# Constant rows of a packed attention operand: from fill transfers to the evacuation itself, for the first two head groups

## The chip, the cores and the metric

One core of a Trainium2 chip runs the kernel. The metric is the device time of one execution in microseconds (us). Executions that the records call fast are compared with fast ones only.

How a ratio is computed: it is the mean time of one kernel's fast runs over that of the kernel before's fast runs of the same rounds, so it is not quite the ratio of the medians that are quoted.

Engines: PE is TensorE (PEld its weight loads), ACT is ScalarE, DVE is VectorE, POOL is GpSimd, SP is SyncE, which issues all DMA transfers here (SPq is its queue).

## The reference, cut to what matters

```python
# S = 2048 tokens, D = 512, H = 32 heads of 16, F = 1792
def reference(A_x, A_wqkv, A_wo, B_x, B_w1, B_w3, B_w2):
    ...
    xn = _layernorm(A_x)
    return A_x + _A_ref(xn, A_wqkv, A_wo) + _B_ref(xn, B_w1, B_w3, B_w2)
# _A_ref: softmax attention over 2048 x 2048 scores in each of 32 heads, then the output projection wo
# _B_ref: the gated feed-forward part (FFN): (silu(xn w1) * (xn w3)) w2
```

The expensive part is 32 x 2048 x 2048 exponentials. They come in 2,048 *score tiles*, each of 128 keys by 512 queries of one head.

## The kernel before

**Layout.** Each head has 16 dimensions, but the matmuls of this kernel take their rows in places of 32. So the transposed keys `KT` and queries `QT` keep four heads in 128 rows: in each place of 32, rows 0 to 15 hold the head, row 16 a constant (1 in `QT`, an offset `YB` in `KT`), and rows 17 to 31 zeros. There are eight such groups of four heads. The offset lets DVE make an exponential out of integer bit operations. ACT makes the other exponentials, three tiles at a time. About a fifth of the tiles (398 of 2,048) go to DVE.

**Fills.** Constants and zeros get into their rows by DMA, from small source rows:

```python
        P.dma(lambda e: e.dma_start(KT[16:128:32, :, :]..., crow[:, 1, :].unsqueeze(1).broadcast_to([4, NG * NQC, 512])),
              reads=[("crow",)], writes=[("KTc",)], kb=128)
        def zeros(g0, g1):
            for j in range(4):
                P.dma(lambda e, j=j: e.dma_start(                                        # L1114
                    KT[32 * j + 17:32 * j + 32, g0:g1, :].rearrange("p g (a n) -> p (g a) n", n=512),
                    zrow[:, :].unsqueeze(1).broadcast_to([15, (g1 - g0) * NQC, 512])),
                    reads=[("zrow",)], writes=[("KTz", g) for g in range(g0, g1)], kb=60 * (g1 - g0))
        for j in range(4):
            P.dma(lambda e, j=j: e.dma_start(QT[32 * j + 17:32 * j + 32, :, :], ...      # L1119
        zeros(0, 2)
        P.post("sp", lambda: [zeros(g, g + 2) for g in range(2, NG, 2)], ready=14.0, prio=2)
```

**Packing moves.** A projection computes 128 dense rows, that is, eight heads. DVE copies them to a staging tile `stg`, and eight transfers of 16 rows carry them to their places:

```python
                def moves(hh):
                    for j in range(4):
                        m = P.dma(lambda e, j=j: e.dma_start(dst(hh)[32 * j:32 * j + 16, :],   # L1303
                                      stg[64 * hh + 16 * j:64 * hh + 16 * j + 16, sl, :]), ..., kb=16)
```

**The end of a unit.** A unit is one group of heads with one chunk of 512 queries, 64 score tiles; there are 32. At its end the sums of the exponentials are fetched by a transfer (`Lc`), inverted on DVE (`Rc`), and spread over the rows by more transfers.

```python
            def e1():
                q = P.dma(lambda e: e.dma_start(Lc[:, u, :], U[16:128:32, us, :]), ...)
                P.post("dve", e2, ready=q.end + _LAT, prio=0)
            ...
            def e2():
                q = P.op("dve", lambda e: e.reciprocal(Rc[:, :], Lc[:, u, :]), reads=[("Lc", u)], writes=[("Rc",)],
                         dur=0.25)                                                       # L1760
                P.post("sp", e3, ready=q.end + _LAT, prio=0)
```

**The order.** The program itself places every instruction in its engine's queue, by a list scheduler that works at build time with assumed durations (`dur`) and a clock `P.t` that steps by 0.02 us. A task is put into an engine's queue when the *model* says that its data will have come, and a transfer is assumed to take 0.06 us of the issuing queue:

```python
    def dma(self, fn, reads=(), writes=(), kb=64, name="", eng="sp"):
        op = _Prog.dma(self, fn, reads, writes, name, eng)
        return self._time(op, op.deps, 0.06, 1.9 + kb / 200.0)   # 0.06 us to issue, then latency
    ...
            P.t += 0.02
```

## Time and profile before

| what | value |
|---|---|
| time, median of the first 3 runs | 1001.12 us (999.04 to 1002.58) |
| span of the profiled run, mean granted clock | 998.7 us, 0.898 |
| first score matmul | 44.2 us |
| time at score tile 128 | 152.2 us |
| time at score tile 513 (first of the second query chunk) | 318.1 us |
| tiles 513 to 2048 | 640.2 us |

From the page of the kernel before: busy time by engine, the 40 slices (a digit is a busy share in tenths, for PEclk the granted clock), the chain that ended last, and two rows of the DMA issues (KB each, us from issue to landing).

```profile
span 998.7 us, 21498 instructions
PE 830.9 (83%) x8925; PEld 251.3 (25%) x8925; DVE 761.5 (76%) x1498; ACT 802.8 (80%) x736; POOL 55.0 (6%) x73
...
PE   3264758897987989698989999889999999898991
...
ACT  4233759797998979699998999888898999988940
...
PEclk9595879899987999899996999998886999998996
...
PE 37%; DVE 30%; ACT 13%; DMA 11%; SPq 7%; issue 2%; POOL 0%; DVEq 0%
...
f_KT<-f_stg SPq DMA_DIRECT2D x128, 16.0 KB, 1.8
...
f_KT<-f_mb SPq DMA_DIRECT2D x16, 120.0 KB, 3.4
```

The first six slices, 150 us, are thin on PE and ACT alike. From there on both are 90% full or near it. By windows (start:end and length; busy time with instruction count of PE, PEld, DVE, ACT and POOL; clock; DMA share; GB/s). The trace has no clock record before 16.5 us, and the view counts time without a record as full clock, so the clock of the first 50 us is read too high.

```profile
0.00:50.00 50.00, 15.38 (x158) 6.29 (x162) 20.10 (x52) 15.53 (x16) 11.43 (x39) 0.77 0.40 99
50.00:100.00 50.00, 28.48 (x356) 9.67 (x348) 18.47 (x33) 17.30 (x21) 1.08 (x3) 0.75 0.42 63
150.00:550.00 400.00, 351.45 (x3648) 99.95 (x3646) 335.71 (x661) 357.51 (x326) 20.94 (x15) 0.92 0.24 31
```

The chain of waits of the kernel before says what the early time goes into (start, length, what):

```profile
24.87 3.33 DMA f_KT<-f_mb
28.22 3.34 DMA f_KT<-f_mb
31.58 3.35 DMA f_KT<-f_mb
34.94 0.87 SPq L1114
```

The timeline of the same stretch (start, length, engine, line, operation; in brackets the idle time before it and what ended it) shows who stands behind these transfers:

```profile
24.87 10.94 SPq L1114 DMA_DIRECT2D f_KT<-f_mb  x4
...
35.85 5.02 SPq L1303 DMA_DIRECT2D f_KT<-f_stg  x8
40.92 5.01 SPq L1303 DMA_DIRECT2D f_QT<-f_stg  x8
44.20 1.06 PE L1536 MATMUL ps<-f_QT,f_KT 32*128 32x512 bf16 x5 [20.03 <-DMA f_QT<-f_stg]
...
45.98 27.69 SPq L1114 DMA_DIRECT2D f_KT<-f_mb  x10
```

The keys were staged by 20.5 us, but their eight moves sit in the SP queue behind the zero fills and start at 35.85. Then 16 moves take 10 us of queue. PE is empty for 20 us. After the first scores the next ten fills hold the queue for another 27.7 us.

### The profile page before, as it was taken

How to read it: one execution, taken by the hardware profiler on the slowest of the kernel's cores; microseconds unless marked ns; L12 is line 12 of the kernel's file. 1: busy time of each engine (PE TensorE's matmuls, PEld its weight loads, DVE VectorE, ACT ScalarE, POOL GpSimd, SP SyncE). 2: the span in 40 equal slices, each digit the busy share in tenths (PEclk: the TensorE clock that was granted, in tenths of full speed). 3: DMA queues.
4: the chain of work that ended last, by engine and by line, in shares of the span. 5: the costliest groups of instructions: out<-in, count | busy, mean ns of one | idle time of the engine just before them, and what ended most of it. 6: DMA issues, size and time to landing. Idle time of an engine off the chain costs nothing.

```text
span 998.7 us, 21498 instructions
## 1 busy us (share of the span) xinstructions
PE 830.9 (83%) x8925; PEld 251.3 (25%) x8925; DVE 761.5 (76%) x1498; ACT 802.8 (80%) x736; POOL 55.0 (6%) x73
## 2 busy tenths in 40 slices
PE   3264758897987989698989999889999999898991
PEld 1021212222221232122221222222222222222261
DVE  5243759797898778598988969878898889886942
ACT  4233759797998979699998999888898999988940
POOL 3100001000000000000000000000000000000000
PEclk9595879899987999899996999998886999998996
DMA  5234322140321222231511131413321222333112
GB/s 161 38 43 81 95 34 39 20 57 23 51 21 9 22 23 35 33 45 24 68 16 6 11 37 17 42 36 52 44 29 12 29 23 30 43 43 46 16 24 31
DMA packets 93294, 37.67 MB, mean 38 GB/s; under 512 B 74756, under 2 KB 91140, under 8 KB 93188
## 3 DMA queue, kind: packets, MB, share of 16 engines
q1 hardware_dynamic: 93188, 36.21, 26.1%
q8 instruction: 72, 1.18, 0.5%
q14 instruction: 34, 0.28, 0.1%
HBM read 22.81 MB, written 2.10 MB: 25 GB/s over the span
## 4 chain that ended last, share of the span: by engine, by line
PE 37%; DVE 30%; ACT 13%; DMA 11%; SPq 7%; issue 2%; POOL 0%; DVEq 0%
PE ps L1536 13%; PE ps L1228 13%; ACT f_PT L1573 12%; PE ps L1725 11%; DVE f_yb L1623 10%; SPq L1303 6%; DVE f_xd L1668 5%; DMA f_KT<-f_mb 4%; DVE f_mb L1657 3%; DVE f_xd L1651 3%; DVE f_xd L1662 3%; DVE f_t L1370 2%; DMA f_Lc<-f_U 2%; DMA f_QT<-f_mb 1%; DVE f_hT L1380 1%
## 5 line engine op out<-in xcount | busy, mean ns | idle before, releaser
L1573 ACT ACTIVATE f_PT<-ps 128x1536 bf16<-128x1536 f32 (+1 forms) x660 | 767.0, 1292 | 134.9 <-PE ps L1536 126.3
L1536 PE MATMUL ps<-f_QT,f_KT 32*128 32x512 bf16 x2048 | 336.7, 412 | 86.2 <-DVE f_yb L1623 26.4
L1623 DVE TENSOR_SCALAR f_yb<-ps 128x512 int16<-128x512 f32 x398 | 271.5, 684 | 58.2 <-PE ps L1536 54.8
L1725 PE MATMUL ps<-f_PT,f_Vaug 128*32 128x512 bf16 (+1 forms) x1650 | 267.6, 413 | 10.2 <-DVE f_xd L1651 5.9
L1725 PE MATMUL ps<-f_xd,f_Vaug 128*32 128x512 bf16 (+1 forms) x1194 | 250.8, 417 | 4.3 <-DVE f_xd L1651 3.2
L1536 PEld LDWEIGHTS ps<-f_QT,f_KT 32*128 32x128 bf16 x2048 | 84.3, 92 | 389.3 <-ACT f_PT L1573 153.9
L1228 PE MATMUL ps<-f_xnT,f_w 128*32 128x512 bf16 x1792 | 150.8, 405 | 29.9 <-DMA f_w<-in_B_w_dram 17.8
L1668 DVE TENSOR_TENSOR f_xd<-f_yb,f_mb 128x1024 bf16<-128x1024 bf16 x199 | 141.3, 713 | 0.0
L1657 DVE TENSOR_SCALAR f_mb<-f_yb 128x1024 int16<-128x1024 int16 x199 | 88.1, 443 | 5.9
L1778 POOL TENSOR_TENSOR f_onorm<-f_U,f_R 128x512 bf16<-128x512 f32 x31 | 42.5, 1372 | 858.4 <-DMA f_R<-f_Rrow 395.2
L1725 PEld LDWEIGHTS ps<-f_PT,f_Vaug 128*32 128x32 bf16 (+1 forms) x1650 | 65.2, 97 | 86.6 <-issue 46.1
L1662 DVE TENSOR_SCALAR f_xd<-f_yb 128x1024 int16<-128x1024 int16 x199 | 86.8, 436 | 0.1
L1651 DVE TENSOR_SCALAR f_xd<-f_yb 128x1024 int16<-128x1024 int16 x199 | 86.6, 435 | 0.0
L1725 PEld LDWEIGHTS ps<-f_xd,f_Vaug 128*32 128x32 bf16 (+1 forms) x1194 | 60.9, 98 | 61.7 <-issue 36.5
L1228 PE MATMUL ps<-f_w,f_hT 128*32 128x512 bf16 x896 | 68.7, 383 | 0.2 <-DVE f_yb L1623 0.2
L1228 PEld LDWEIGHTS ps<-f_xnT,f_w 128*32 128x32 bf16 x1792 | 39.5, 96 | 100.5 <-issue 65.7
L1380 DVE SCALAR_TENSOR_TENSOR f_hT<-f_t,ps 128x512 bf16<-128x512 bf16 x56 | 38.1, 680 | 17.4 <-PE ps L1228 16.9
L1228 PE MATMUL ps<-f_wo,f_onorm 128*32 128x512 bf16 x512 | 41.4, 391 | 8.8 <-DVE f_onorm L1778 8.8
L1370 DVE SCALAR_TENSOR_TENSOR f_t<-f_th,ps 128x512 bf16<-128x512 f32 x56 | 38.1, 680 | 11.9 <-ACT f_th L1366 11.7
L1366 ACT ACTIVATE f_th<-ps 128x512 f32<-128x512 f32 x56 | 35.9, 641 | 1.2 <-PE ps L1228 1.2
L1246 DVE CAST f_Vaug<-ps 128x512 bf16<-128x512 f32 x16 | 10.9, 688 | 29.6 <-PE ps L1228 29.6
L1228 PEld LDWEIGHTS ps<-f_w,f_hT 128*32 128x32 bf16 x896 | 25.7, 95 | 24.3 <-issue 17.0
(49 smaller groups left out, 230.8 us busy)
## 6 DMA issues: line engine op xcount, KB each, us to landing
f_w<-in_B_w_dram SPq DMA_DIRECT2D x112, 128.0 KB, 3.9
f_R<-f_Rrow SPq DMA_DIRECT2D x128, 32.0 KB, 4.4
f_KT<-f_stg SPq DMA_DIRECT2D x128, 16.0 KB, 1.8
f_QT<-f_stg SPq DMA_DIRECT2D x128, 16.0 KB, 1.8
f_xr<-in_A_x_dram SPq DMA_DIRECT2D x16, 128.0 KB
out_dram<-f_xn_sb SPq DMA_DIRECT2D x16, 128.0 KB, 1.7
f_KT<-f_mb SPq DMA_DIRECT2D x16, 120.0 KB, 3.4
f_w<-in_B_w_dram SPq DMA_DIRECT2D x1, 1792.0 KB
```

The source lines that it names most:

```text
L1228: ins = e.matmul(bank(bk)[32 * i:32 * i + 32, 0:ncols], make_lhsT(i), rhs_ap, start=start, stop=stop, tile_position=(0, 32 * i))
L1303: m = P.dma(lambda e, j=j: e.dma_start(dst(hh)[32 * j:32 * j + 16, :], stg[64 * hh + 16 * j:64 * hh + 16 * j + 16, sl, :]), reads=[("stg", ...
L1370: q2 = P.op("dve", lambda e: e.scalar_tensor_tensor(t1[:, ss, :], th[:, ss, :], 1.0, bank(bk), ALU.add, ALU.mult), reads=[("th", ss), ("ps ...
L1380: q = P.op("dve", lambda e: e.scalar_tensor_tensor(hT[:, fc, :], t1[:, ss, :], 0.5, bank(bk), ALU.mult, ALU.mult), reads=[("t1", ss), ("ps ...
L1536: ins = e.matmul(bank(b), l_, r_, start=True, stop=True, tile_position=(rp, 0))
L1573: q = P.op("act", lambda e: e.activation(PT[:, p0:p0 + w, :].rearrange("p a n -> p (a n)"), ps[:, b0 * 512:(b0 + w) * 512], ACTF.Exp, scal ...
L1623: q = P.op("dve", lambda e: e.tensor_scalar(yb[:, ys, 512 * h:512 * h + 512], bank(bk), 0.0, 32767.0, ALU.max, ALU.min), reads=[("ps", bk) ...
L1651: q_ = P.op("dve", lambda e: e.tensor_scalar(dsl[:, s_, 0, :], yb[:, ys, :], 0x7F80, None, ALU.bitwise_and), reads=YK, writes=[("ds", s_, ...
L1657: P.op("dve", lambda e: e.tensor_scalar(mb[:, ys, :], yb[:, ys, :], 0x7F, 0x3F00, ALU.bitwise_and, ALU.bitwise_or), reads=YK, writes=[("mb ...
L1662: q_ = P.op("dve", lambda e: e.tensor_scalar(dsl[:, s_, 1, :], yb[:, ys, :], -352.0, 0.0, ALU.add, ALU.max), reads=YK, writes=[("ds", s_, ...
L1668: q_ = P.op("dve", lambda e: e.tensor_tensor(dsl[:, s_, 2, :].bitcast(BF16), yb[:, ys, :].bitcast(BF16), mb[:, ys, :].bitcast(BF16), ALU.m ...
L1725: ins = e.matmul(bank(PV)[32 * j:32 * j + v_.shape[-1], :], v_, p_, start=s0, stop=s1, tile_position=(0, 32 * j))
```

## The change

Its intent is to get rid of that queue at the start. (1) The projections of head groups 0 and 1 no longer compute dense rows. A column set of the weights is taken 32 wide at a stride of 16, so PSUM already has each head in its 32-row place (the other 16 rows hold a neighbour's values), and the copy out of PSUM multiplies by a per-row mask and adds a per-row constant. (2) All other constant rows are filled by ACT and DVE. (3) The weights are loaded in parts, the columns of groups 0 and 1 first, and tokens are laid out p-major (a partition holds 16 consecutive tokens). (4) The LayerNorm chain on POOL has two steps for a pair of tiles in place of four.

```diff
-        x_v = A_x[0].rearrange("(t p) d -> p t d", p=128)
+        x_v = A_x[0].rearrange("(p t) d -> p t d", t=NT)
 ...
-        P.dma(... QT[16:128:32, :, :] <- crow ...)        # and all zeros(...): 22 fill DMAs
+        P.op("dve", ... tensor_reduce(rowc[:, 0:1], ident[:, 16:128:32], AX.X, ALU.add) ...)   # 1 at row 16 of a place
+        # rowc 1 = 1 - rowc 0;  rowc 2 = QS at rows 0..15;  rowc 3 = YB at row 16
+        fill_a(QT[:, 2:4, :]..., 0, ...)                   # ACT: groups that still use packing moves
+        fill_a(KT[:, 2, :], 3, ...)
+        def fills():                                       # DVE, about 26 us in the scheduler's time
+            for g in range(3, NG):
+                P.op("dve", ... tensor_scalar(KT[:, g, :], src, 0.0, rowc[:, 3:4], ALU.mult, ALU.add) ...)
 ...
+        def direct(dst, key, dkey, mul, add, eng):
+            ...        # dst = PSUM * rowc[:, mul] + rowc[:, add], on ACT or DVE
+        def spread(w, key, g, s0):
+            ...        # lhsT = w[:, c, 64 * g + 16 * q : 64 * g + 16 * q + 32]
 ...
-            order.append(tile_KT(0, gi))
+            order.append(tile_K1(0, gi))
             if gi == 0:
-                order.append(tile_QT(0, 0))
+                order.append(tile_Q1(0))
 ...
+        for sc in range(NQC):
+            crit.append((16 + 10 * sc, k, tile_K1(1, sc)))
 ...
-                P.op("pool", lambda e: e.tensor_tensor(lnt[:, sl_], mv[:, sl_, 0], lnr[:, sl_], ALU.mult), ...)
-                o = P.op("pool", lambda e: e.tensor_scalar(lnb[:, sl_], lnt[:, sl_], -1.0, 0.0, ALU.mult, ALU.add), ...)
```

The places of the direct query projection are zero in rows 17 to 31, so what the keys have there does not count. Some smaller edits, not shown, go with it: a score group for ACT is placed only when its PSUM banks are idle in the model, the first value projections wait for the keys, and the late weight loads start after the fills. The rest of the program text is nearly the same, but the scheduler runs over all of it: every later instruction may get another place.

## The prediction

> **What bounds the kernel now.** Between 150 and 950 us three engines are nearly full (busy time by windows: PE about 93%, ACT 92%, DVE 85%), and score tiles run at about 2.4 per us (1,918 score matmuls in 800 us). The first 150 us hold only 131 score tiles, worth about 55 us at that rate. The timeline shows why: the first score matmul starts at 44.2 us, only 15 run before 83.4 us, and PE is empty in 30-40 and 70-80 us. The chain of waits runs there almost only through fill DMAs (zeros into QT from 9.3 us, into KT in 25-35 and 46-80 us) and the packing moves behind them in the same in-order queue. A KT fill moves 120 KB in 3.4 us, 36 GB/s. The Trainium skill ("DMA: Bandwidth & Descriptors", Rules for kernel authors) says that an outermost dimension below 16 confines a transfer to that many engines; here it is 15 or 4, and the slow landing agrees. The granted clock is 0.50 in the empty stretches, as the skill ("TensorE: Matmul & The Clock Gate", What's actually happening) says of an idle array.
>
> **Removed.** All 22 fill DMAs, 40 packing moves of groups 0 and 1 (0.59 us of queue each), 6.6 us of ACT fills, two of four POOL steps of the LayerNorm chain (0.4 us a pair). The first scores need only 160 columns of wk and wq, but on PE they stand behind the first V tile, so still wait for wv.
>
> **Added.** 20 more groups of projection matmuls (0.25 us each, 5 us of PE), two ACT fills before the first evacuation (2.8 us, hidden by the load), on DVE two memsets, five KT fills and one wo fill (scaled from 0.43 us for 1,024 elements: some 6 us in all). The instruction order shows about 17 exponentials moved from DVE to ACT (0.46 us per tile: 8 us of ACT).
>
> **On the critical path.** Before, the first V matmul ran at 12.4 us, when wv had landed. Less data is now ahead of wv (1.9 against 2.5 MB), so I expect the first score at 12-14 us in place of 44. From there projections, LayerNorm and fills (40-odd us of DVE) share the time with scores made by ACT alone: about 55 score tiles at 60 us, which before were reached near 110 us. By 513 score tiles both orders have done the same FFN work. Costing that stretch by engine gives 250-260 us (ACT 220 us of work, DVE 218, PE 205, at 0.90 density after a 13 us start), plus 5-10 us of stalls that I expect to remain: packing moves of groups 2 and 3 in one queue, and the normalisation chain behind them, like the holes at 105 and 130 us. Before, 513 tiles were reached near 310 us. The rest is the same work at the same rate; the tail from 975 us (24 us, last normalisation and output) is untouched.
>
> **Prediction.** A gain of about 50 us: 950 us, range 931 to 969. Faster by over 2%: 0.96; within 2%: 0.03; slower: 0.01.
>
> **Right if** the timeline shows the first score at 12-14 us, no empty 10 us slice before 100 us, no fill DMA in the chain, granted clock near 0.9 from 20 us on, 2.4 score tiles per us later. **Wrong if** p-major or 320-byte weight rows make loads land late, the DVE fills near 30 us stop PE, the packing queue stalls scores before tile 128 for 10 us or more, or the re-made schedule loses later or in the tail.

## The result and the profile after

The changed kernel took 962.7 us (median of 4 runs, 958.57 to 968.58), the kernel before 1001.85 us (median of 4, 999.04 to 1003.4). The ratio of the fast runs is 0.9617, 95% interval 0.9557 to 0.9676. The profiled execution was the slowest of the four, span 966.8 us.

The same views of the page, of the changed kernel:

```profile
span 966.8 us, 21462 instructions
PE 840.2 (87%) x8973; PEld 243.4 (25%) x8973; DVE 750.1 (78%) x1464; ACT 808.8 (84%) x743; POOL 50.6 (5%) x57
...
PE   6897886999999999869799999988889988979892
...
ACT  5697786999989799867899899999899797979840
...
PEclk9999797999779999887879999999779997979596
...
PE 41%; DVE 27%; ACT 18%; SPq 6%; DMA 5%; issue 2%; POOL 0%; DVEq 0%
```

And its windows:

```profile
0.00:50.00 50.00, 36.01 (x406) 13.70 (x406) 34.24 (x74) 32.43 (x36) 8.61 (x26) 0.97 0.51 132
50.00:100.00 50.00, 41.86 (x498) 12.67 (x498) 34.84 (x61) 40.47 (x37) 1.26 (x1) 0.97 0.13 17
150.00:550.00 400.00, 358.46 (x3737) 100.24 (x3729) 324.10 (x629) 351.60 (x320) 19.78 (x15) 0.90 0.24 31
```

The start is what the change was for: PE is busy 36 of the first 50 us against 15, and the clock is read as 0.97 against 0.77. If the time without a record ran at half clock in both, as the slow matmuls there suggest, these would be 0.80 and 0.60 (our estimate). The fills are gone from the chain, whose DMA share fell from 11% to 5%. But between 150 and 550 us ACT is now busy *less* in 400 us than before (351.6 against 357.5), and its row of slices has 678 in places 18 to 20 and 979797 in places 31 to 36, where the kernel before had 999 and 899998.

The timeline of the new start (the first three rows are the projections of keys, queries and the first values; the fifth is the first scores):

```profile
11.24 1.90 PE L1235 MATMUL ps<-f_xnT,f_wkv 128*32 128x512 bf16 x16 [0.84 <-ACT f_xnT L1274]
12.89 1.94 PE L1235 MATMUL ps<-f_xnT,f_wq 128*32 128x512 bf16 x16
14.60 1.94 PE L1235 MATMUL ps<-f_wkv,f_xnT 128*32 128x512 bf16 x16
14.89 0.78 ACT L1348 ACTIVATE f_QT<-ps,f_rowc 128x512 bf16<-128x512 f32 x1 [3.79 <-PE ps L1235]
16.48 0.91 PE L1581 MATMUL ps<-f_QT,f_KT 32*128 32x512 bf16 x5
```

**Where the time came from, and where part of it went again.** The start of the Nth score matmul, in us, counted from the traces:

```
tile            1     64    128    513    768   1025   1536   2048    end
before       44.2  115.4  152.2  318.1  429.9  534.4  748.2  958.3  998.7
after        16.5   61.6   92.1  266.8  372.7  494.5  701.3  929.7  966.8
lead         27.7   53.8   60.1   51.3   57.2   39.9   46.9   28.6   31.9
```

The lead is 60 us at tile 128 and still 51 us at tile 513. Of that, 22.7 us are lost between tile 513 and tile 2048 (640.2 us before, 662.9 after), where both kernels have nearly the same work: 6,276 matmul records before and 6,310 after. The tail gives 3.3 us back: 51.3 - 22.7 + 3.3 = 31.9. (The 34 matmuls that after does more in the stretch it has less in the tail.) So two questions are open: which part of the change made the early lead, and what took the 20 us later.

### The profile page after: what moved, and what is told of

The parts are those of the page before. It is cut to its first block, busy times and chain, and to the rows that moved or that the text cites. A ratio compares the mean times of both kernels' runs of the same rounds, so it can differ in the third digit from the quotient of the medians.

```text
span 966.8 us, 21462 instructions
## 1 busy us (share of the span) xinstructions
PE 840.2 (87%) x8973; PEld 243.4 (25%) x8973; DVE 750.1 (78%) x1464; ACT 808.8 (84%) x743; POOL 50.6 (5%) x57
## 4 chain that ended last, share of the span: by engine, by line
PE 41%; DVE 27%; ACT 18%; SPq 6%; DMA 5%; issue 2%; POOL 0%; DVEq 0%
ACT f_PT L1620 16%; PE ps L1235 16%; PE ps L1581 14%; PE ps L1772 11%; DVE f_yb L1670 9%; SPq L1310 5%; DVE f_xd L1715 4%; DVE f_mb L1704 3%; DVE f_xd L1698 3%; DVE f_xd L1709 2%; DMA f_Lc<-f_U 2%; DVE f_hT L1420 1%; DVE f_t L1410 1%; DMA f_w<-in_B_w_dram 1%; DVE f_stg L1302 1%
## 5 line engine op out<-in xcount | busy, mean ns | idle before, releaser
L1620 ACT ACTIVATE f_PT<-ps 128x1536 bf16<-128x1536 f32 (+1 forms) x667 | 775.8, 1286 | 108.9 <-PE ps L1581 89.7
L1670 DVE TENSOR_SCALAR f_yb<-ps 128x512 int16<-128x512 f32 x382 | 259.2, 682 | 47.7 <-PE ps L1581 44.7
L1772 PE MATMUL ps<-f_xd,f_Vaug 128*32 128x512 bf16 (+1 forms) x1146 | 246.7, 427 | 5.2 <-DVE f_xd L1698 4.4
L1235 PE MATMUL ps<-f_xnT,f_w 128*32 128x512 bf16 x1792 | 155.7, 407 | 25.4 <-DMA f_w<-in_B_w_dram 14.4
L1581 PEld LDWEIGHTS ps<-f_QT,f_KT 32*128 32x128 bf16 x2048 | 81.8, 92 | 360.4 <-ACT f_PT L1620 172.0
L1715 DVE TENSOR_TENSOR f_xd<-f_yb,f_mb 128x1024 bf16<-128x1024 bf16 x191 | 135.0, 708 | 0.0
L1698 DVE TENSOR_SCALAR f_xd<-f_yb 128x1024 int16<-128x1024 int16 x191 | 83.4, 437 | 0.0
L1709 DVE TENSOR_SCALAR f_xd<-f_yb 128x1024 int16<-128x1024 int16 x191 | 83.1, 435 | 0.1
L1772 PEld LDWEIGHTS ps<-f_xd,f_Vaug 128*32 128x32 bf16 (+1 forms) x1146 | 58.5, 98 | 61.9 <-issue 32.0
L1468 DVE TENSOR_TENSOR f_xn_sb<-ps,f_xr 128x512 bf16<-128x512 f32 x12 | 8.2, 687 | 32.5 <-PE ps L1235 32.5
L1807 DVE RECIPROCAL f_Rc<-f_Lc 128x16 f32<-128x16 f32 x32 | 7.9, 246 | 29.6 <-DMA f_Lc<-f_U 29.6
```

Source lines behind the costliest of these rows:

```text
L1235: ins = e.matmul(bank(bk)[32 * i:32 * i + 32, 0:ncols], make_lhsT(i), rhs_ap, start=start, stop=stop, tile_position=(0, 32 * i))
L1581: ins = e.matmul(bank(b), l_, r_, start=True, stop=True, tile_position=(rp, 0))
L1620: q = P.op("act", lambda e: e.activation(PT[:, p0:p0 + w, :].rearrange("p a n -> p (a n)"), ps[:, b0 * 512:(b0 + w) * 512], ACTF.Exp, scal ...
L1670: q = P.op("dve", lambda e: e.tensor_scalar(yb[:, ys, 512 * h:512 * h + 512], bank(bk), 0.0, 32767.0, ALU.max, ALU.min), reads=[("ps", bk) ...
L1698: q_ = P.op("dve", lambda e: e.tensor_scalar(dsl[:, s_, 0, :], yb[:, ys, :], 0x7F80, None, ALU.bitwise_and), reads=YK, writes=[("ds", s_, ...
L1709: q_ = P.op("dve", lambda e: e.tensor_scalar(dsl[:, s_, 1, :], yb[:, ys, :], -352.0, 0.0, ALU.add, ALU.max), reads=YK, writes=[("ds", s_, ...
```

## The experiments

The early lead was tested by undoing or doing alone one part of the change. For the late loss these theories were set against each other; the texts on record name some of them by letter and spell them out:

- *Half clock*: PE runs part of the stretch at half clock because its mix of work is thin in dense projection groups there; the order decides how they are spread.
- *A lucky order before*: the order that the scheduler made for the kernel before was an especially good one, any new order loses.
- *A VectorE wait*: DVE takes its queue in order (see a_pow below), so when it stands at one instruction whose data are late, all behind it stand too, and PE runs dry.

Two readings of our own serve all experiments. The first is the time at a tile, as above. The second takes the stretch from tile 513 to tile 2048: its length, the time DVE stood before a reciprocal (`Rc`) there, the idle time of PE in gaps of over 2 us, and PE's busy time while the clock was low. All are in us, from the profiled run of each kernel:

```
kernel        length   DVE wait at Rc (longest)   PE gaps > 2 us   PE busy at low clock
before         640.2      5.0  (2.6)                  15.8               78.5
b_step21       627.6      4.0  (3.0)                   8.7               82.8
b_fill         656.5     18.9  (5.7)                  29.3               78.9
b_pace         640.8     21.2  (6.1)                  26.6               44.0
after          662.9     19.6  (6.1)                  23.6              116.3
after_again    659.5     19.6  (6.0)                  26.4               89.6
a_tmajor       654.6     19.7  (6.0)                  26.6               87.8
a_pack         658.5     14.4  (6.0)                  25.8              100.1
a_step21       638.1      4.9  (3.8)                   9.4               89.4
a_pace2        623.9      6.0  (5.4)                   7.1               22.7
a_pow          629.1      0.0  (0.0)                   6.1               66.3
best1          614.5      0.0  (0.0)                   8.1                8.9
```

Names that begin with b_ are edits of the kernel before, names with a_ of the changed kernel.

### after_again: the changed kernel, unedited, in five rounds

> The changed kernel once more, unedited. In its first profile it was 51 us ahead of the kernel before at score tile 513 and 57 at tile 768, but only 28 us ahead at tile 2,048: about 23 us were lost in the middle. Theory C (clock): the loss comes from stretches at half the granted clock, whose sum differs from run to run (160 us of PE busy time in such stretches against 135 in the kernel before); then the median is 960 to 964 us, single runs differ by about 1%, and in the new profile the lead at tile 2,048 moves with the time spent at low clock. Rival S (schedule): the re-made instruction order is worse in the middle; then the same 20-odd us are lost between the same tiles again, whatever the clock.

Measured: 963.29 us (962.31 to 965.25, 6 runs) against 1000.73 us of the kernel before (11 runs), ratio 0.9641 (0.9606 to 0.9677). The stretch from tile 513 took 659.5 us with 27 us less of PE's busy time at low clock than in the first profile of the same kernel. So the late loss repeats (19.3 us), and in the same places, tiles 768 to 1025 and 1536 to 2048: that was the rival's forecast. A good part of the low clock in the first profile of after was that run's own: the 27 us more of low clock went with 3.4 us of length.

### b_fill: the kernel before with the engine fills, packing moves kept

```diff
-        (all 22 fill DMAs, zrow, crow, the ACT fills of wo, R, Vaug)
+        fill_a(QT[:, 0:4, :]..., 0, ...)
+        for g_ in range(2):
+            fill_a(KT[:, g_, :], 3, ...)
+        def fills(): ...            # KT groups 2..7 and wo on DVE
```

> The kernel before with one part of the change: constant rows written by ACT, DVE and POOL instead of fill DMAs; packing moves for all groups, whole weight loads, token order and the four-step LayerNorm chain stay. If the fill DMAs in front of the packing moves are the main cause, the first score comes at 21 to 26 us (in place of 44, the packing moves of K and Q, 16 issues of 0.59 us, stay in front of it), and 60 to 85% of the gain is there: 968 to 978 us. Rival (the packing moves and the evacuation straight into place matter most): first score after 32 us and under half of the gain, over 982 us.

Measured: 982.84 us (977.4 to 991.71, 4 runs), ratio 0.9861 (0.9803 to 0.9919). The time lies 5 us above the expected 968 to 978 us, on the rival's side of its own line (982), and the first score came at 29.5 us, later than expected: the load of wv still held PE for 3.3 us, and the packing moves of group 0 for 6.9 us. At tile 128 this kernel is at 110.0 us, 42 us ahead of the kernel before, and at tile 513 at 281.0, 37 us ahead. At the end only 18 us are left of that (by the medians). The loss after tile 513 is there too, 16 us, in a kernel without direct projection, p-major or the new LayerNorm. What it shares with the changed kernel in the second table is the DVE wait, 18.9 us.

### a_pack: the changed kernel with groups 0 and 1 packed by transfers again

```diff
-        fill_a(QT[:, 2:4, :]..., 0, ...)
-        fill_a(KT[:, 2, :], 3, ...)
+        fill_a(QT[:, 0:4, :]..., 0, ...)
+        for g_ in range(2):
+            fill_a(KT[:, g_, :], 3, ...)
 ...
-            order.append(tile_K1(0, gi))
+            order.append(tile_KT(0, gi))
```

> The changed kernel with one part undone: groups 0 and 1 are projected for 64 rows and brought into place by packing moves again; no fill DMAs, split weight loads, p-major tokens and the short LayerNorm chain stay. If the direct projection is worth what its 40 removed moves cost on the way to the first score (16 issues of 0.59 us and a landing of 2 us, less the evacuation that stays), the first score comes 8 to 11 us later than in the changed kernel, at 25 to 28 us, and the total is 4 to 12 us longer: 966 to 975 us. Rival (PE has other work meanwhile, so it is hidden): within 3 us of the changed kernel.

Measured: 986.51 to 1006.23 us in 4 runs, two of them slow, so without an interval; the two fast ones took 986.51 and 998.73. The changed kernel took 963.3 on the same chip, so the direct projection is worth 23 to 35 us inside this kernel, against the 4 to 12 that were expected. The expectation counted the first group's moves only. The first score is late by 9 us (24.5), but PE also stands 8.2 us at 43.5 for the key moves of the next 512 keys, 7.6 us at 96 behind DVE and 10.7 us at 156 for a staging tile. The kernel needs the keys of group 0 four times, 512 keys each, and each time they stand in the queue. The late stretch (658.5) is as bad as in after, so the late loss does not need the direct projection.

### a_tmajor: the changed kernel with the old token layout

```diff
-        x_v = A_x[0].rearrange("(p t) d -> p t d", t=NT)
-        out_v = out[0].rearrange("(p t) d -> p t d", t=NT)
+        x_v = A_x[0].rearrange("(t p) d -> p t d", p=128)
+        out_v = out[0].rearrange("(t p) d -> p t d", p=128)
```

> The changed kernel with tokens t-major again (1 KB in place of 2 KB and more of contiguous bytes per partition in the x loads); the instruction order is the same. Expected: x lands at most 0.5 us later, first score within 1 us of 16.5 us, total the same within noise (less than 4 us). Rival: the layout matters for the load phase, and the first score comes over 1.5 us later.

Measured: 964.2 us (958.29 to 968.16, 4 runs), ratio 0.9641 (0.9586 to 0.9697), as after_again. The order of instructions is the same as in after, so this is also one more repeat of that order. The first score starts at 15.9 us against 15.7. The p-major layout is worth nothing that these runs can see, in loads or in the order.

### a_noffn: the changed kernel with the FFN left out (a wrong result)

```diff
-            if part != 2:
+            if False:                                  # no w2 groups
 ...
-            for fc in range(FC):
-                bg.extend(tiles_FFN(sc, fc))
```

> The changed kernel without its FFN (wrong result on purpose): no G, Y and hidden-to-output matmuls, no tanh; only scores, PV, projections and the attention part of the output are left, about 40% less PE busy time. Two readings of the half-clock stretches in the middle. Theory D (drought): the long ones hold no dense matmul groups at all (FFN, projection, output), only score and PV matmuls that alternate, and such a mix does not bring the clock back up; then this kernel stays at half clock for most of the span (mean granted clock under 0.65), makes about 2.0 score tiles per us, and ends at 1,030 to 1,110 us, later than with the FFN. Rival: half-clock stretches come from waits alone; then with less work PE waits for ACT, about 2.5 tiles per us, granted clock near 0.9, 870 to 910 us.

Measured: one run, of unknown state, 920.41 us, span 918.7, mean clock 0.768. (It passed the comparison with the reference: the FFN's share of the output is smaller than the tolerance.) Of the matmuls between tiles 513 and 2048 31% are gone (4,357 records against 6,310), yet tiles 513 to 2048 still took 632 us: PE was busy at low clock for 300 us of them. This fits the reading that a PE which has only scores and value products to do gets half the clock for long. But both forecasts missed: the clock fell less than theory D expected (0.768, 2.43 score tiles per us), and the kernel became faster, where D expected 1,030 us or more and the rival 870 to 910. It does not show that low clock made the 20 us: here a PE at low clock has room to spare.

The same can be seen in the changed kernel. In this window PE is busy 18.99 of 20 us at a clock of 0.50. Of the 120 matmuls that start in it only 16, that is 13%, are of projections or the FFN; in the whole kernel it is 45% (4,048 of 8,973):

```profile
900.00:920.00 20.00, 18.99 (x123) 3.50 (x120) 17.58 (x36) 17.68 (x16) 0.89 (x1) 0.50 0.24 21
```

### b_step21 and a_step21: the order re-made, nothing else

```diff
-            P.t += 0.02
+            P.t += 0.021
```

The scheduler's clock steps a little wider. The program is the same, its order is made anew. One thing moves with the order: how many exponentials DVE makes (398 becomes 386 in the kernel before, 382 becomes 376 in the changed one).

> The kernel before with one number of its scheduler changed that has no meaning for the hardware: the step of its model time, 0.021 in place of 0.02. The instruction mix stays, the order comes out different. All re-made orders so far took 655 to 663 us from score tile 513 to tile 2,048, and the kernel before 640. Theory L (the order of the kernel before is an especially good one, as its constants were tuned on it): this kernel also needs 650 to 665 us there, and 1,008 to 1,025 us in all. Rival (the change itself, in its later scheduling rules or group layout, makes the middle slower): 636 to 645 us there, total within 5 us of the kernel before.

> The changed kernel with the same meaningless number changed (0.021 in place of 0.02). Its early phase should stay as it is (score tile 128 at 89 to 95 us). Theory L: the middle, tile 513 to 2,048, lands anywhere in 645 to 668 us, so the total in 948 to 976 us. Rival: it repeats the 655 to 663 us and the total stays in 958 to 967 us.

Measured: b_step21 987.22 us (985.29 to 993.88, 4 runs), ratio 0.9891 (0.9826 to 0.9955); a_step21 948.5 us (944.13 to 956.27, 6 runs), ratio 0.9488 (0.9441 to 0.9536). Both are *faster* than what they were made from, by 11 and 15 us. Their stretches are shorter than either side had forecast. The theory of an especially lucky order before has fallen: another order is better still. The smaller scheduling edits of the change do not force the loss either, for a_step21 has them all. What stands is that a re-made order alone moves the time by 11 to 15 us, and that it does so in the late stretch (640 to 628, and 660 to 638). The second table says with what: the DVE wait is 4 to 5 us in the three kernels with a good stretch and 14 to 20 in b_fill and the four kernels of the changed kind with a bad one, while the low clock is about the same, 79 to 90, in a_step21, b_fill and after_again. The split of the exponentials does not sort the kernels like this: of those made by DVE, 290 fall in this stretch in a_step21 and in b_pace (below, 21 us of waits), 298 in before and in after.

### a_pace2 and b_pace: the FFN's groups spread evenly over the score tiles

```diff
+        def due(sc, n):
+            return 512 * sc + (100 if sc == 0 else 90) + (4.0 if sc == 0 else 3.6 if sc == NQC - 1 else 4.0) * n
 ...
-                        [("w13", sl, which)] + xk(sc * 512, 512), None, DG))
+                        [("w13", sl, which)] + xk(sc * 512, 512),
+                        lambda n=8 * fc + 4 * which + c: st["pos"] >= due(sc, n), DG))
```

> The changed kernel with its FFN matmul groups spread over the score tiles: a group may start only when the count of score tiles has come to its due place (4 tiles per group; in the last quarter 3.6). Theory D: with dense groups in every stretch PE spends much less busy time at half clock (under 90 us in place of 137 to 159), tile 513 to 2,048 takes at most 648 us, total 940 to 955 us. Rival (waits and not droughts set the clock, and a scheduler that holds work back loses): low-clock time as before, total 962 us or more.

> The kernel before with the same spreading of its FFN groups over the score tiles, and nothing of the change. If the half-clock droughts cost time in any order of this program, the middle (tile 513 to 2,048, 640 us before) falls to 618 to 632 us with under 40 us of PE busy time at low clock (78 before), and the total to 975 to 990 us, so that the change and the spreading add up (936 us with both). Rival (spreading only repairs what the change broke): total 993 us or more.

Measured: a_pace2 936.43 us (933.94 to 941.71, 4 runs), ratio 0.9381 (0.9323 to 0.944). b_pace 1009.1 us (1008.79 to 1011.22, 4 runs), ratio 1.0096 (1.0059 to 1.0133). The spreading did to the clock what it should in both: the low-clock time of the stretch fell from 90 to 23 and from 78 to 44 us. But only one became faster. In a_pace2 the DVE waits had fallen too, from 19.6 to 6.0; in b_pace they rose from 5.0 to 21.2, the stretch kept its length (640.8), and 8 us were lost before tile 513. So b_pace fell on its rival's side (993 us or more), the half clock alone is not the cause, and what a_pace2 gained is not the spreading's alone.

### a_pace_pow: the spread version once more

The kernel is a_pace2, unedited.

> The spread version once more, one look: first score at 15 to 17 us, tile 128 at 89 to 93 us, under 90 us of PE busy time at low clock, 930 to 945 us.

Measured: one run, 938.55 us, with 6.1 us of DVE wait in the stretch. It repeats a_pace2.

### a_pow: the reciprocal moved from DVE to POOL, nothing else

This tests the DVE wait directly. The waits of DVE for the transfer of the sums (total us, times, longest us), in the whole of the kernel before and of the changed one:

```profile
DVE f_Rc L1760 <- DMA f_Lc<-f_U: 27.2, 7, 9.5
...
DVE f_Rc L1807 <- DMA f_Lc<-f_U: 29.6, 10, 6.1
```

The sums differ little; what differs is where they lie: 5.0 us of the first and 19.6 of the second come after tile 513. One of the latter, from SP's timeline, then DVE's, then PE's:

```profile
407.77 4.96 SPq L1310 DMA_DIRECT2D f_QT<-f_stg  x8
412.78 0.58 SPq L1218 DMA_DIRECT2D f_w<-in_B_w_dram  x1
413.40 0.51 SPq L1220 DMA_DIRECT2D f_w<-in_B_w_dram  x1
413.95 0.61 SPq L1795 DMA_DIRECT2D f_Lc<-f_U  x1
...
416.00 0.25 DVE L1807 RECIPROCAL f_Rc<-f_Lc 128x16 f32<-128x16 f32 x1 [5.34 <-DMA f_Lc<-f_U]
...
416.86 0.60 PE L1581 MATMUL ps<-f_QT,f_KT 32*128 32x512 bf16 x1 [5.00 <-DVE f_t L1410]
417.39 0.61 PE L1772 MATMUL ps<-f_PT,f_Vaug 128*32 128x512 bf16 x1
```

The sums were in `U` at 408.3 us, after its copy on DVE. Their transfer was issued at 413.95, behind eight packing moves (4.96 us, 0.62 each) and two weight loads, and the scheduler had counted 0.06 us for each of these. So it put the reciprocal into DVE's queue some 5 us too early. DVE stood 5.34 us at an instruction of 0.25 us, and PE ran dry for 5.00 us; what released it is DVE's next instruction, which reads PSUM and so frees a bank. Then PE comes back at 0.61 us for a matmul that took 0.39 before the hole: the hole also costs the clock, whose record turns to 0.50 at 416.5 us. In the changed kernel the four DVE-made gaps of PE in this stretch (5.00, 2.41, 3.21 and 5.83 us) all end just after a reciprocal with such a wait, and they are 16.5 of its 23.6 us of gaps over 2 us; the other three end with a weight load. Counted over the 24 transfers of sums in the stretch, five are issued more than 2 us after the sums are in `U` in the changed kernel, two in the kernel before and one in a_step21; packing moves of queries stand before each of the late ones in the first two, and weight loads too before two.

That ScalarE, VectorE and GpSimd take their queues strictly in order is what the Trainium skill states ("TensorE: Matmul & The Clock Gate", the table at its head, row Engine queue depth), and the 5.34 us agree. On SP, the skill ("Perfetto Trace Analysis", What "DMA-bound" means) says that an issuing engine whose track is solid with transfers is bound by making descriptors and not by moving data. This trace agrees: the 11 issues from 407.77 to 414.56 follow each other with less than 0.1 us between them.

```diff
+        mone = sb("mone", [128, 16], FP32)                 # filled with -1
-                P.post("dve", e2, ready=q.end + _LAT, prio=0)
+                P.post("pool" if u < NU - 1 else "dve", e2, ready=q.end + _LAT, prio=0)
 ...
+                if u < NU - 1:
+                    q = P.op("pool", lambda e: e.tensor_tensor(Rc[:, :], Lc[:, u, :], mone[:, :], ALU.pow), ..., dur=1.0)
```

POOL has little else to do, so it may stand.

> The changed kernel with one edit: the reciprocal of the attention sums is formed on GpSimd (as the power -1) instead of on VectorE; nothing of the pacing, the start or the scheduler's step is touched. Theory W (the late loss is VectorE standing in order at the reciprocal until the transfer of the sums lands, and TensorE running dry behind it): the waits of VectorE for that transfer, 29.6 us in ten waits in the changed kernel, go; the gaps of over 2 us on TensorE between tile 513 and tile 2048 fall from 24-26 us to 10 or less; that stretch falls from 659-663 us to 632-645; the whole to 940-952 us. Rival C (the half-clock stretches, or the luck of a re-made order, are the cause and the reciprocal's place matters little): the stretch stays at 652 or more and the whole at 957 or more. 952 to 957 would leave both partly open.

Measured: 929.24 us (927.31 to 931.36, 4 runs), ratio 0.9321 (0.929 to 0.9353), which is 34 us below the changed kernel (32 by the ratios, as the two ran on different chips) and better than the expectation. The wait has moved to POOL, where it costs nothing that the chain shows (POOL has 0% of it; its 418.5 us are mostly time in which it had nothing to do). What is left on DVE is the last unit, whose reciprocal stayed there:

```profile
DVE f_Rc L1813 <- DMA f_Lc<-f_U: 1.9, 1, 1.9
...
POOL f_Rc L1810 <- DMA f_Lc<-f_U: 418.5, 31, 31.2
```

The stretch from tile 513 fell from 659.5 to 629.1 us, PE's gaps from 26.4 to 6.1 us, and the low clock, which nothing had touched on purpose, from 89.6 to 66.3. Three of the 24 transfers of sums are still issued over 2 us late here, and DVE no longer waits for them. The rival, that the reciprocal's place matters little, expected 652 us or more and is out. One thing limits the reading. Moving an instruction re-makes the order as well (the DVE queues of the two kernels part after 92 instructions of some 1,460), and a_step21 gained 15 us by that alone. But a_step21's own gain came with a DVE wait of 4.9 us in place of 19.6, so it points to the same cause. How much of the 34 us is the new order's own stays open.

### best1: everything that had helped, together

This is a_pace2 with the reciprocal on POOL and a mended start: 60 matmuls without use at the start of PE's queue, the LayerNorm statistics taken pair by pair, and the first value projection after the first scores.

```diff
+        def warm(e):
+            for i in range(60):
+                ins = e.matmul(bank(7)[:, 0:128], ident[:, :], ones_t[:, :], start=True, stop=True)
+            return ins
 ...
-                    P.post("dve", one, ready=0.0, prio=3)
+                    P.post("dve", one, ready=0.0, prio=2)
 ...
-                cond=lambda: ("K0_%d" % (t // 4)) in done and xc())
+                cond=lambda: ("K0_%d" % (t // 4)) in done and xc() and st["pos"] > 0)
 ...            # and the edits of a_pace2 and a_pow
```

> The spread version with two more edits. One: the reciprocal of the row sums moves from DVE to POOL (as a power of -1), for all units but the last, since DVE stood 28 us in front of it, in holes of up to 6.6 us, waiting for a small DMA. Two, at the start: 60 unused matmuls from about 1.5 us on, to have the clock up when the first projections come (they ran at 0.43 us per group, 0.25 us later), the statistics of tokens' tiles 0 and 1 finished before those of 2 and 3, and the first V tile after the first scores. Expected: first score at 11 to 13 us in place of 15.8, DVE waits for that DMA gone, 12 to 22 us saved in all, 914 to 926 us. Rival (the holes are filled by work that other engines had waiting, and the early gain is used up by V and the projections): 930 to 938 us.

Measured: 909.96 us (908.54 to 918.92, 4 runs), ratio 0.9127 (0.9071 to 0.9184), with correct results. It beats both kernels, the changed one by 53 us. Its PE timeline at the start:

```profile
1.41 5.00 PE L1113 MATMUL ps<-f_ones_t,f_ident 128*128 128x128 bf16 x60 [1.41 <-POOL f_mone L1106]
...
10.89 1.05 PE L1242 MATMUL ps<-f_xnT,f_wkv 128*32 128x512 bf16 x16 [0.94 <-ACT f_xnT L1281]
...
13.68 0.60 PE L1592 MATMUL ps<-f_QT,f_KT 32*128 32x512 bf16 x5 [0.88 <-ACT f_QT L1355]
```

The 16 matmuls of the first key projection take 1.05 us here against 1.90 in the changed kernel (the first clock record, of full clock, is at 4.6 us here), and the first score comes 2.0 us earlier than in after_again. Against a_pow this kernel is 18.8 us shorter in the profiled spans: 3.3 by tile 128, 14.6 between tiles 513 and 2048.

**The two costs together.** Four kernels of the second table stand in a square. With waits of 20 us: 659.5 us at 90 us of low clock (after_again), 640.8 at 44 (b_pace). Without waits: 629.1 at 66 (a_pow), 614.5 at 9 (best1). Down the square 26 to 30 us go with the waits, across it 15 to 19 go with the low clock. Each of the four is also an order of its own, and b_pace comes from the kernel before, so these are sizes and not exact shares. All twelve rows together say much the same: the straight-line fit is length = 610 + 1.16 x DVE wait + 0.27 x low clock (our estimate; three of the rows are one order). It leaves 4 us as a rule and 9 at most, in b_step21: before and b_step21 differ by 12.6 us at nearly equal waits and low clock. So the two readings do not explain everything.

## Why the prediction was right or wrong

It said 950 us and the time was 962.7, inside its range, and the sign was right for the reason given. That the number stayed in the range is in part luck: a loss of 19 to 23 us had no term in the sum, and a step of the scheduler's clock that means nothing (a_step21) moves the time by 15 us.

- **The start.** Right. It put tile 55 at 60 us, and the trace has it at 55.6. No slice is empty, no fill is left in the chain, and the clock is 0.97 from 50 to 100 us.
- **The first score at 12 to 14 us.** It came at 16.5 and 15.7 us. The prediction costed the first projections at the usual 0.25 us per group, but they ran at half clock: 1.90 us in place of 1.05 for the keys' set of 16, and 1.94 for each of the next two. A projection matmul takes 0.63 us up to the first clock record, of full clock, at 17.1 us, and 0.38 right after it; in after_again the same step comes at 14.8 us, and the first score 0.8 us earlier. The shorter LayerNorm chain gave nothing here. Its POOL steps are fewer, but in the new order the first normalisation starts at 7.83 us, against 6.86 before, because the statistics of the second pair are mixed in between those of the first. best1, with both mended and the first value projection moved behind the scores, has the first score at 13.68.
- **Tile 513 at 255 to 270 us, before near 310.** Measured 266.8 and 318.1. The lead of 51 us at this point is the gain of about 50 that was predicted for the whole (the kernel before came 8 us later here than the prediction had it).
- **Which part pays.** The prediction did not divide it. Engine fills alone give 42 us at tile 128 and 37 at tile 513 (b_fill). With them in place the rest of the change, the direct projection above all, adds 14 to 17 us at tile 513 (b_fill at 281.0, after at 266.8 and 264.3). The direct projection alone, taken away from after, costs 35 to 37 us there (a_pack at 301.5). The parts do not add up to a plain sum. p-major gives nothing that was measurable.
- **Cost on ACT.** Right. About 17 exponentials were to move to ACT for 8 us; they cost 8.8 (767.0 to 775.8 us of exponentials), DVE making 382 in place of 398.
- **The step that failed: "The rest is the same work at the same rate".** The work was the same within 1%, the rate was not: 2.40 score tiles per us before (1,535 in 640.2 us), 2.32 after (in 662.9). The prediction had the right warning in its last line ("the re-made schedule loses later"), but gave it no term in the sum. The runs put in its place a loss of 19 to 23 us that follows the order of the instructions and not the parts of the change: b_fill loses 16 us without most of them, a_step21, with all of them, loses nothing against the kernel before (but 10 us against b_step21). The new order has 19.6 us of DVE waits at the reciprocal in this stretch where the old one had 5.0, because the transfer of the sums more often falls behind packing moves and weight loads in SP's queue (five late issues of 24 against two). By the fit above these waits are worth 17 us. Taking this wait off DVE, with the new order that comes with it, returns 30 us of the stretch and 34 of the whole.
- **The half clock** is real and costs on its own, but in the difference of the two kernels it is at most a smaller part (3 to 10 us by the fit): it is 78.5 us in the kernel before, and in the changed one 116.3 in the first profile and 89.6 in the second, with nearly the same loss.

What stays open: why just this order has the sums' transfer behind more issues than the one before, other than that the scheduler counts 0.06 us for what takes ten times as long; what else makes up the 12.6 us between before and b_step21; whether a right figure there would do the same as moving the reciprocal; and what moving it would give the kernel before, which has 27.2 us of such waits in all but only 5.0 after tile 513. None of these was run.

## What to carry to other kernels

A transfer that is cheap in bytes is not cheap in an in-order queue: count issues as well as bytes, and put constant rows into the evacuation that has to run anyway. When a change makes a program-wide order anew, give the untouched stretch a term and a width of its own in the prediction, and afterwards compare time at equal *work done* and not at equal time. Let an engine that is nearly full never stand in order for a transfer: give the tiny instruction behind the transfer to an idle engine, even if it runs twelve times longer there (3.03 us on POOL against 0.25 on DVE).

## What the Trainium skill lacked or had wrong

- "TensorE: Matmul & The Clock Gate" (What's actually happening) says that a sustained busy window of about 3.4 us releases the full clock. The two states of 0.50 and 1.00 agree, and so does the half clock after holes. But PE was busy 18.99 of 20 us in the window from 900 us and stayed at 0.50, with no gap over 0.5 us; leaving the FFN out brought the mean clock from 0.90 to 0.768 (one run). The page does not say that a PE which is nearly always busy with small score and value matmuls can stay at half clock for 20 us; its passage on cycling through PSUM banks comes nearest and speaks of short idles and oscillation.
- The same page (Seeing it yourself) warns that clock events in a trace can be unreliable. No run here shows a wrong event. What the page lacks is that a trace can have no clock record at all at its start: the changed kernel's begins at 17.1 us, our view prints 1.00 for 11 to 16 us, and 16 matmuls took 1.90 us there, against 1.05 after a warm-up.
- "DMA: Bandwidth & Descriptors" (Anatomy of one DMA) gives about 50 ns for the sequencer's part of a DMA on the GpSimd path. For the path from SP the page has a latency to the first byte and, in a part on trn3, a count of sequencer cycles for "previous generations". It has no measured issue time of a small transfer between SBUF places from SP, which is what counts here: 0.62 us each, eight in 4.96 us.
- "GPSIMD Engine Reference" has no figure for a power on POOL: 3.03 us for 128x16 elements in fp32, against 0.245 us for DVE's reciprocal of the same size.
